# Attention stage: read-outs loaded 14 places behind their store, maxima sent by ScalarE from group 10 on, segment rows loaded one by one, more masks by VectorE

## The chip, the core and the metric

The kernel runs on one core of one Trainium2 chip. The core has TensorE (matrix products), VectorE, ScalarE, GpSimd and SyncE, each with an instruction queue of its own that is worked through in order. SyncE does nothing but issue DMAs; ScalarE can issue them as well. The metric is the device time of one execution in microseconds. Before the change the median of three runs was 810.78 us (809.48 to 811.25).

## The reference

A transformer block over 2048 tokens of width 512: a conditioned layer norm, attention with 32 heads of 16 elements in four segments of 512 tokens with a memory carried from segment to segment, the output projection with a residual, a second conditioned layer norm and a GELU network of width 1792 with a residual. The attention, cut to what matters:

```python
for s in range(N):                                   # four segments
    qs, ks, vs = q[:, :, s], k[:, :, s], v[:, :, s]
    logits = jnp.einsum("bhqd,bhkd->bhqk", qs, ks) * scale + mask     # causal
    p = _softmax(logits, axis=-1)
    a_dot = jnp.einsum("bhqk,bhkd->bhqd", p, vs)
    num = jnp.einsum("bhld,bhde->bhle", pq, M)
    den = jnp.einsum("bhld,bhd->bhl", pq, z)[..., None] + 1e-6
    o = g * (num / den) + (1.0 - g) * a_dot
    ...
x = x + ga * (o @ wo)
h = _layernorm(x, axis=-1) * (1 + cb) + sb
x = x + gb * _B_ref(h, w1, b1, w2, b2)               # GELU network
```

## The kernel before

The program has three stages: the projections for q, k and v with the memory; the attention (in the trace from about 180 to 505 us), into which the output projection of the first three segments and the first steps of the second layer norm are woven; and the GELU network. The order of the work is written out by hand.

**Groups, rounds and places.** The attention treats the 32 heads of a segment in eight groups of four heads, so there are 32 groups Q, numbered over the four segments. A group is two pairs P of two heads. The loop over the string ORDER makes one round per group; a round has 20 places, c0 to c19, between the score and exponential steps. Work that isn't part of a pair's own steps is put at a place by ap(place, function, arguments), where place 20 x R + n is cn of round R. Two entries of one place run in the order in which they were added.

**A group's own work.** Round R computes the raw scores of group R + 2 (s_part, lines 606 to 645) in six PSUM banks "att", one bank for a head of a pair or for both. VectorE takes the row maxima, either by a pass that adds the causal mask as it goes (masked_max, line 613), or by a plain reduction of both heads at once (line 617), for which TensorE has added the mask by a matmul of its own (line 645). PRM["m"] says by which way the two short score blocks of each pair go, from group 14 on (PRM["mq"]). Round R also computes the transposed scores of group R (st_part, line 693), to which three more rows of the stack qst add the negated maxima, so they can't start before these rows have landed. ScalarE takes the exponential (lines 708 and 719), GpSimd zeroes the masked triangle (line 696), and one round later, at places c11 to c18, TensorE multiplies by V (pv_part, line 733).

**Maxima.** For group Q GpSimd splits the maxima into three bf16 parts (m_rows, line 661, place 20Q - 21), TensorE transposes them (m_put, line 667, place 20Q - 13), ScalarE copies them to ms, and m_send (line 675, place 20Q - 11) issues the DMA into rows 96 to 98 of the group's stack. One exponential of 512 columns stands between m_put and m_send in the order. Group Q needs them at the beginning of round Q, 11 places later. The stacks themselves (kst and qst, line 175) are loaded at place 20Q - 65 into one of four buffers and first used at place 20Q - 40.

**Read-outs.** The result of group Q is copied to ts (ScalarE) and stored to TD at place 20Q + 42 (line 751). Two groups make a read-out U: it is loaded back in another layout at place 40U + 69, 7 places behind the second store (pv_in: dn, opk, from segment 1 on amB, in segment 3 also rm; lines 756 to 770). The divisor is inverted and scaled at 40U + 84 (den, lines 775 and 776), stored to RD at +88 (line 784), and loaded as a broadcast rbB at +96 (rb_in, line 788). At +107 the mixing multiplies and adds (lines 793 and 795, GpSimd up to read-out 12), at +117 ScalarE copies the high part (o_hi, line 127 with tile oh), at +119 GpSimd makes the low part (o_lo, line 810). Read-outs 6 and 10 make both parts 16 places later, the last two read-outs have times of their own. TensorE projects the result (wo_part, line 821) from place 242 on, two parts a round in rounds 12 to 27, four in rounds 28 to 31. VectorE adds the residual (line 839), or ScalarE and GpSimd do (line 837); the sum X2D is stored 6 places later (line 847).

**Second layer norm.** For segments 0 and 1 the four blocks of X2D are loaded again (ln2_load, line 556), measured on VectorE (561, 562), given their factor on GpSimd (148, 149), normalised (568; GpSimd in segment 0, VectorE in segment 1) and turned by TensorE (574). In segment 0 the four loads stand together at place 400, 8 places behind the last store (392); the normalisations stand at 454, 464, 474 and 484, the four turns at 493, 503, 513 and 523.

**DMAs.** All DMAs of this stage are issued by SyncE, in the order of their places; one that has to wait holds all behind it. In the order of the program the eight DMA semaphores are used in turn.

Of the kernel before, what the change touches and what calls it, by code (L numbers as in the profile page):

```python
# [27 lines left out]
PRM = {'turn': 2,  # L28
 'pv': [[31, 0, 0, 512], [36, 1, 128, 512], [37, 2, 256, 512], [38, 3, 384, 512]],
 'pvlast': [[25, 0, 0, 512], [30, 1, 128, 512], [31, 3, 384, 512], [35, 2, 256, 512]],  # L30
 'mrows': -21,
 'mput': -13,
 'stacks': -65,
 'den': [84, 84, 84, 84],
 'dnl': 11,
 'rbl': 12,
 'rdl': 4,
 'tsl': 4,
 'msl': 2,
 'xol': 6,  # L40
 'mix': 107,
 'ohi': 117,
 'olo': 119,
 'end': {'rbl': 7, 'mix': 103, 'ohi': 111, 'olo': 116},
 'wo': [[20 * i + o for i in range(8) for o in (2, 5)]] * 2 + [[20 * i + o for i in range(4) for o in (2, 5, 8, 14)]],
 'wox': -25,
 'olate': 16,
 'mixu': 13,
 'olou': 13,
 'ht': [493, 503, 513, 523],  # L50
 'ht1': 644,
 'ln': [[400, 413, 449, 454], [531, 566, 603, 624]],
 'lnl': [0, 4, 20, 34],
 'wl': [26, 66, 80, 81],
 'gate': 197,
# [18 lines left out]
 're': 'v',  # L74
 'am3': 1,
 'rme': 'p',
 'mmix': 88,
 'lnd': [[11, 10], [10, 2]],
 'mp': 0,
 'wout': ['vvvv', 'vava', 'vvvv'],  # L80
 'dens': ['p', 'p', 'p', 'v'],
 'm': [0, 0, 0, 1],
 'mq': 14,
 'pvo': ['a', 'a'],
 'mse': 'a',
# [16 lines left out]
def block_kernel(ctx: ExitStack, tc: tile.TileContext, x, wq, wk, wv, wo, betaq, betam,  # L102
                 w1, b1c, w2, b2, ccol, wmod, maskbd, mask8, out):
    nc = tc.nc
    v, act, pool, pe, sp = nc.vector, nc.scalar, nc.gpsimd, nc.tensor, nc.sync
# [57 lines left out]
    NK = 4  # L163
    qst, kst = {}, {}
# [419 lines left out]
    with ExitStack() as pb:  # L584
# [87 lines left out]
        mss = {}  # L672

        def m_send(Q):
            sp.dma_start(qst[Q % NK][96:99], mss.pop(Q))

        pts = {}
        late = []
# [227 lines left out]
        def at(P, part, f, *a):  # L906
            todo.setdefault((P, part), []).append((f, a))
# [23 lines left out]
        def ap(pos, f, *a):  # L931
            at(pos // 10, pos % 10, f, *a)
# [20 lines left out]
        for U in range(16):  # L953
            z = U // 4
            ap(40 * U + 20 + PRM["pv"][3][0] + PRM["dnl"], pv_in, U)
            if U == 15:
                ap(40 * U + 20 + PRM["pv"][3][0] + PRM["dnl"], am_in, U)
            p = {**PRM, **PRM["end"]} if U > 13 else PRM
            den_at = 40 * U + PRM["den"][z]
            ap(den_at, den, U)  # L960
            if U < 14:
                ap(den_at + PRM["rdl"], den_store, U)
            ap(den_at + p["rbl"] + (5 if U == 14 else 0), rb_in, U)
            assert 20 + PRM["pv"][3][0] + PRM["dnl"] <= PRM["den"][z] and PRM["den"][z] + p["rbl"] <= p["mix"]
            ap(40 * U + PRM["mmix"], mem_mix, U)
            ap(40 * U + p["mix"], mix, U)
            assert PRM["mmix"] <= p["mix"]
            late_by = PRM["olate"] if U in (6, 10) else 0
            ap(40 * U + p["ohi"] + late_by, o_hi, U)
            ap(40 * U + p["olo"] + late_by, o_lo, U)  # L970
            assert PRM["den"][z] <= p["mix"] <= p["ohi"] <= p["olo"]
        for s in range(NSEG - 1):
            for b in range(4):
                w = [160 * s + 240 + i for i in PRM["wo"][s][4 * b:4 * b + 4]]
# [6 lines left out]
                    ap(w[3] + 1 + PRM["xol"], wo_store, s, b)  # L981
        assert all(y[0] <= x <= y[3] < 0 for y in PRM["vl"] for x in y)
        assert PRM["wl"] == sorted(PRM["wl"]) and PRM["gate"] > PRM["wl"][1] + 60
        for i, (ln, ld) in enumerate(zip(PRM["ln"], PRM["lnd"])):
            assert ln[0] + PRM["lnl"][3] * i > 160 * i + 241 + PRM["wo"][i][15] and ln[1] > ln[0]
            assert ln[1] + 3 * ld[0] < ln[2] < ln[3] and ln[3] + 3 * ld[1] < (PRM["ht"][0], PRM["ht1"])[i]
        assert PRM["ln"][1][0] > PRM["ht"][3] and PRM["ht"] == sorted(PRM["ht"])
        def gate_load():
            sp.dma_start(gab, modD[5:6, :].to_broadcast([128, D]))

# [3 lines left out]
        at(-1, 9, swap)  # L994

        ap(PRM["gate"], gate_load)
        for i, (ln, ld) in enumerate(zip(PRM["ln"], PRM["lnd"])):
            for b in range(4):
                ap(ln[0] + PRM["lnl"][b] * i, ln2_load, i, b)
                ap(ln[1] + ld[0] * b, ln2_stats, i, b)  # L1000
                ap(ln[3] + ld[1] * b, ln2_apply, i, b, (pool, v)[i])
            ap(ln[2], ln2_rstd, i)
        for j in range(2):
            for i in range(4):
                ap(PRM["wsub"][j] + i, w_sub, j, i, v)
# [422 lines left out]
```

## Time and profile before

| | us |
|---|---|
| median of three runs | 810.78 (809.48 to 811.25) |
| the profiled execution, device time | 808.31 |
| its span, first to last instruction | 806.6 |
| TensorE busy in the span | 778.6 |
| VectorE / ScalarE / GpSimd busy | 553.5 / 476.2 / 331.8 |
| DMA queue of SyncE, share of 16 engines | 60.9% |

A page of the profile gives the busy time of each engine, slices of the span, the chain of work that ended last, and the costliest groups of instructions by line. The views named in the prediction: a list of waits (engine, line and tile that waited, what ended the wait; total us, how often, longest), stretches (busy us of each engine between two times, then the granted clock, the DMA share and GB/s), the chain of work (start, us, what), the timeline (start, us, engine, line, operation, out<-in, how many; in brackets the idle time before and what ended it), and groups by line (busy us, mean ns, idle time before). PE is TensorE, PEld its weight loads, DVE VectorE, ACT ScalarE, POOL GpSimd, SPq and ACTq the issuing of DMAs by SyncE and ScalarE. L675 is line 675 of the kernel. The end of a matmul is modelled.

### The profile page before, as it was taken

The page shows a single profiled execution, that of the slowest core. Times are in us where ns is not written, and L with a number is a line of the kernel's source. Part 1 is how long each engine was busy: PE and PEld are TensorE (multiplying, and loading weights), DVE is VectorE, ACT ScalarE, POOL GpSimd, SP SyncE. Part 2 cuts the span into 40 slices and gives each one's busy share as a digit, 9 for nine tenths or more (in the row PEclk, how much of TensorE's full clock was granted, in tenths as well). Part 3 has the DMA queues.
Part 4 walks back from the last instruction along what each step waited for, and adds up shares of the span by engine and source line. Part 5 has one row for each costly group of instructions (what it writes and reads, how often), then busy time and mean ns, then how long its engine had stood idle before and what let it go on. Part 6 is the DMA issues. An engine that isn't in the chain of part 4 may idle for free.

```text
span 806.6 us, 14065 instructions
## 1 busy us (share of the span) xinstructions
PE 778.6 (97%) x4631; PEld 539.2 (67%) x4631; DVE 553.5 (69%) x1275; ACT 476.2 (59%) x910; POOL 331.8 (41%) x554
## 2 busy tenths in 40 slices
PE   8999999999999999998989798989999999999998
PEld 4877767876545455554545455768888888888887
DVE  6686697458888877876867687867668866632523
ACT  4465545465888877775777475757745336653221
POOL 1347266451578655565875485133000404400000
PEclk9999999999999999999999999899999999999999
DMA  9596857395555667767657764585575744445443
GB/s 338 179 320 230 277 181 238 142 328 175 169 165 164 189 191 197 194 174 224 173 173 200 196 175 135 166 266 170 203 252 165 221 135 154 161 143 165 157 136 117
DMA packets 108817, 156.09 MB, mean 194 GB/s; under 512 B 16324, under 2 KB 55620, under 8 KB 108744
## 3 DMA queue, kind: packets, MB, share of 16 engines
q1 hardware_dynamic: 107880, 153.63, 60.9%
q10 hardware_dynamic: 864, 1.57, 0.5%
q8 instruction: 36, 0.59, 0.3%
q14 instruction: 37, 0.30, 0.1%
HBM read 93.95 MB, written 60.83 MB: 192 GB/s over the span
## 4 chain that ended last, share of the span: by engine, by line
PE 74%; DMA 7%; DVE 6%; ACT 4%; POOL 4%; issue 3%; SPq 1%; ACTq 0%; DVEq 0%; POOLq 0%
PE bx L1080 8%; PE att L693 7%; PE pv L733 7%; PE q L313 5%; PE bx L1345 5%; PE att L606 5%; PE by L1345 4%; PE bv L1345 4%; PE k L313 4%; PE bv L1080 4%; PE mm L821 3%; PE v L464 3%; PE spare L1345 2%; PE by L1080 2%; DMA qst<-ms 2%
## 5 line engine op out<-in xcount | busy, mean ns | idle before, releaser
L613 DVE CUSTOM_DVE_ANT_0 dump<-att,maskb 128x512 bf16<-128x512 f32 (+1 forms) x292 | 159.4, 595 | 44.6 <-PE att L606 22.0
L708 ACT ACTIVATE pt<-att 128x384 f32<-128x384 f32 (+1 forms) x256 | 124.8, 544 | 24.6 <-PE att L693 21.2
L696 POOL TENSOR_SCALAR_AFFINE_SELECT pt<-pt 128x256 f32<-128x256 f32 x256 | 103.2, 421 | 74.3 <-ACT pt L708 59.3
L693 PE MATMUL att<-qst,kst 99*128 99x256 bf16 (+3 forms) x512 | 108.3, 302 | 7.6 <-DMA qst<-ms 5.7
L693 PEld LDWEIGHTS <-kst 99*128 99x128 bf16 x512 | 43.8, 98 | 71.8 <-issue 35.9
L865 POOL TENSOR_TENSOR wb<-wa 128x256 f32<-128x256 f32 x24 | 21.4, 894 | 154.9 <-DMA wa<-in_w 144.3
L606 PE MATMUL att<-kst,qst 96*128 96x512 bf16 (+1 forms) x292 | 76.5, 344 | 3.9 <-DMA qst<-QD 3.3
L733 PE MATMUL pv<-pt,V 128*32 128x512 f32 (+1 forms) x992 | 79.6, 439 | 0.0
L719 ACT ACTIVATE pt<-att 128x256 f32<-128x256 f32 (+1 forms) x128 | 62.7, 493 | 23.2 <-PE att L693 22.7
L617 DVE TENSOR_REDUCE nm<-att 128x2 f32<-128x256 f32 (+1 forms) x110 | 56.4, 534 | 15.0 <-PE att L645 11.6
L136 DVE TENSOR_TENSOR gl<-s,gh 128x512 fp32r<-128x512 f32 x34 | 23.7, 697 | 42.1 <-ACT gh L133 42.1
L733 PEld LDWEIGHTS pv<-pt,V 128*32 128x32 f32 x992 | 25.9, 109 | 36.2 <-issue 28.1
L133 ACT ACTIVATE gh<-s 128x512 fp32r<-128x512 f32 x34 | 21.3, 628 | 46.3 <-PE spare L1345 16.7
L1085 ACT ACTIVATE s<-s,b1t 128x512 f32<-128x512 f32 x42 | 30.2, 720 | 17.9 <-DVE s L1089 17.9
L1089 DVE TENSOR_TENSOR s<-bv,s 128x512 f32<-128x512 f32 x28 | 19.2, 687 | 24.4 <-PE bv L1080 19.0
L606 PEld LDWEIGHTS <-qst 96*128 96x128 bf16 x292 | 23.7, 98 | 13.6 <-issue 7.6
L509 POOL TENSOR_TENSOR q<-qr,q 128x512 bf16<-128x512 f32 x16 | 18.7, 1168 | 27.8 <-ACT q L508 27.5
L645 PE MATMUL att<-maskb,identb 128*128 128x256 bf16 x110 | 29.9, 278 | 0.0
L500 POOL TENSOR_SCALAR qp<-qp 128x512 f32<-128x512 f32 x12 | 18.8, 1563 | 25.8 <-ACT qp L495 25.8
L136 DVE TENSOR_TENSOR w1ml<-s,w1mh 128x512 fp32r<-128x512 f32 x18 | 13.0, 721 | 22.5 <-ACT w1mh L133 22.5
L643 PE MATMUL att<-kst,qst 96*128 96x128 bf16 (+1 forms) x110 | 27.3, 248 | 0.8 <-ACT pt L708 0.8
L133 ACT ACTIVATE w1mh<-s 128x512 fp32r<-128x512 f32 x18 | 11.3, 629 | 26.8 <-PE spare L1345 11.3
(364 smaller groups left out, 2152.0 us busy)
## 6 DMA issues: line engine op xcount, KB each, us to landing
GD<-s SPq DMA_DIRECT2D x56, 256.0 KB
s<-GD SPq DMA_DIRECT2D x52, 256.0 KB
kst<-KD SPq DMA_DIRECT2D x32, 384.0 KB
qst<-QD SPq DMA_DIRECT2D x32, 384.0 KB
TD<-ts SPq DMA_DIRECT2D x32, 256.0 KB
xt<-X2D SPq DMA_DIRECT2D x28, 256.0 KB
wa<-in_w SPq DMA_DIRECT2D x28, 256.0 KB
QD<-q SPq DMA_DIRECT2D x16, 384.0 KB
```

The lines of the kernel that those rows point to most:

```text
L136: lo_eng.tensor_tensor(out=lo, in0=src, in1=hi.bitcast(F32), op=ALU.subtract)
L313: pe.matmul(ps, a[:, k, 128 * g:128 * g + 128], b[k], start=(k == 0 and i == 0), stop=(k == KB - 1 and i == 2))
L606: pe.matmul(ps, q_of(P, h, i), k_of(P, h, 128 * (i + 1)), start=True, stop=True)
L613: v.tensor_tensor_reduce(out=dump[n_dump[0] % 2][:, :n], in0=src, in1=maskb[:, 512 - n:], scale=-1.0, scalar=-4 * NEG, op0=ALU.add, op1=AL ...
L617: v.tensor_reduce(out=dst, in_=src, axis=AX.X, op=ALU.max, negate=True)
L693: pe.matmul(ps, k[:99, e, 128 * j:128 * j + 128], q[:99, e, 128 * j:512], start=True, stop=True)
L696: pool.affine_select(out=t, in_=t, pattern=pattern, compare_op=ALU.is_ge, fill=0.0, base=0, channel_multiplier=-1)
L708: act.activation(pt[:, h, :], ps[:, :n], AF.Exp, scale=0.25)
L719: act.activation(pt, pv_, AF.Exp, scale=0.25)
L733: pe.matmul(ps[32 * c:32 * c + 32, lo:hi], V[4 * s + j][:, VW * hd:VW * hd + 32], pt[:, c % 2, lo - o:hi - o], start=start, stop=stop)
L1080: pe.matmul(ps, a[:, i, k, :], b[k], start=start and k == 0 and c == 0, stop=k == 1 and c == 2, skip_group_check=not start)
L1345: pe.matmul(ps, a[:, c], w[:, lo:hi], start=(f == 0 and i == 0), stop=(last and i == 2))
```

## The change

Four things, all in the attention stage; what is computed stays the same.

1. Read-outs 0 to 10 and 12 move back: load at 40U + 76, divisor at +92, its store at +96, broadcast at +110, mixing at +120, high and low part at +130 and +132, the product with rm (mem_mix) at +100. Read-outs 11 and 13 keep the old places ("quick"), the last two theirs ("end"). The extra delay of read-outs 6 and 10 is gone. So the broadcasts of read-outs 10 and 12 (places 510 and 590) stand directly behind the loads of read-outs 11 and 13 (509 and 589).
2. From group 10 on ScalarE issues m_send, at the same place.
3. The X2D blocks of segment 0 are loaded at 388, 397, 408 and 417, measured at 420, 427, 434 and 446 (413, 424, 435, 446 before), normalised at 460, 467, 481 and 487, and turned at 498, 506, 514 and 523. For segment 1 the loads go from 531, 535, 551 and 565 to 528, 537, 548 and 568.
4. From group 14 on the score block of 256 columns of a group's first pair goes by masked_max as well, as that of the second pair did: two passes of 256 columns, no mask matmul, no reduction.

```diff
--- before.py
+++ after.py
@@ -31,26 +31,27 @@
- 'den': [84, 84, 84, 84],
- 'dnl': 11,
- 'rbl': 12,
+ 'den': 92,
+ 'dnl': 18,
+ 'rbl': 18,
  'rdl': 4,
  'tsl': 4,
  'msl': 2,
+ 'msa': 10,
  'xol': 6,
- 'mix': 107,
- 'ohi': 117,
- 'olo': 119,
- 'end': {'rbl': 7, 'mix': 103, 'ohi': 111, 'olo': 116},
+ 'mix': 120,
+ 'ohi': 130,
+ 'olo': 132,
+ 'quick': {'dnl': 11, 'den': 84, 'rbl': 12, 'mix': 107, 'ohi': 117, 'olo': 119},
+ 'end': {'dnl': 11, 'den': 84, 'rbl': 7, 'mix': 103, 'ohi': 111, 'olo': 116},
...
- 'olate': 16,
- 'ht': [493, 503, 513, 523],
+ 'ht': [498, 506, 514, 523],
- 'ln': [[400, 413, 449, 454], [531, 566, 603, 624]],
- 'lnl': [0, 4, 20, 34],
+ 'ln': [{'in': [388, 397, 408, 417], 'stat': [420, 427, 434, 446], 'rstd': 449, 'on': [460, 467, 481, 487]},
+        {'in': [528, 537, 548, 568], 'stat': [566, 576, 586, 596], 'rstd': 603, 'on': [624, 626, 628, 630]}],
...
- 'mmix': 88,
- 'lnd': [[11, 10], [10, 2]],
+ 'mmix': 100,
- 'm': [0, 0, 0, 1],
+ 'm': [0, 1, 0, 1],
@@ -672,7 +672,7 @@
         def m_send(Q):
-            sp.dma_start(qst[Q % NK][96:99], mss.pop(Q))
+            (sp if Q < PRM["msa"] else act).dma_start(qst[Q % NK][96:99], mss.pop(Q))
@@ -952,23 +952,22 @@
         for U in range(16):
-            ap(40 * U + 20 + PRM["pv"][3][0] + PRM["dnl"], pv_in, U)
+            p = {**PRM, **(PRM["end"] if U > 13 else PRM["quick"] if U in (11, 13) else {})}
+            in_at, den_at = 40 * U + 20 + PRM["pv"][3][0] + p["dnl"], 40 * U + p["den"]
+            ap(in_at, pv_in, U)
...
-            p = {**PRM, **PRM["end"]} if U > 13 else PRM
-            den_at = 40 * U + PRM["den"][z]
             ap(den_at, den, U)
             if U < 14:
                 ap(den_at + PRM["rdl"], den_store, U)
             ap(den_at + p["rbl"] + (5 if U == 14 else 0), rb_in, U)
...
-            late_by = PRM["olate"] if U in (6, 10) else 0
-            ap(40 * U + p["ohi"] + late_by, o_hi, U)
-            ap(40 * U + p["olo"] + late_by, o_lo, U)
+            ap(40 * U + p["ohi"], o_hi, U)
+            ap(40 * U + p["olo"], o_lo, U)
@@ -994,12 +994,12 @@
-        for i, (ln, ld) in enumerate(zip(PRM["ln"], PRM["lnd"])):
+        for i, ln in enumerate(PRM["ln"]):
             for b in range(4):
-                ap(ln[0] + PRM["lnl"][b] * i, ln2_load, i, b)
-                ap(ln[1] + ld[0] * b, ln2_stats, i, b)
-                ap(ln[3] + ld[1] * b, ln2_apply, i, b, (pool, v)[i])
-            ap(ln[2], ln2_rstd, i)
+                ap(ln["in"][b], ln2_load, i, b)
+                ap(ln["stat"][b], ln2_stats, i, b)
+                ap(ln["on"][b], ln2_apply, i, b, (pool, v)[i])
+            ap(ln["rstd"], ln2_rstd, i)
```

Lines that only check the order of the places are left out.

More of the change, by code (lines that the diff above doesn't have):

```diff
@@ L954, in block_kernel @@
             z = U // 4
-            ap(40 * U + 20 + PRM["pv"][3][0] + PRM["dnl"], pv_in, U)
+            p = {**PRM, **(PRM["end"] if U > 13 else PRM["quick"] if U in (11, 13) else {})}
+            in_at, den_at = 40 * U + 20 + PRM["pv"][3][0] + p["dnl"], 40 * U + p["den"]
+            ap(in_at, pv_in, U)
             if U == 15:
-                ap(40 * U + 20 + PRM["pv"][3][0] + PRM["dnl"], am_in, U)
-            p = {**PRM, **PRM["end"]} if U > 13 else PRM
-            den_at = 40 * U + PRM["den"][z]
+                ap(in_at, am_in, U)
             ap(den_at, den, U)
@@ L963, in block_kernel @@
             ap(den_at + p["rbl"] + (5 if U == 14 else 0), rb_in, U)
-            assert 20 + PRM["pv"][3][0] + PRM["dnl"] <= PRM["den"][z] and PRM["den"][z] + p["rbl"] <= p["mix"]
-            ap(40 * U + PRM["mmix"], mem_mix, U)
+            assert in_at <= den_at and p["den"] + p["rbl"] <= p["mix"]
+            mm_at = 88 if p["mix"] < 120 else PRM["mmix"]
+            ap(40 * U + mm_at, mem_mix, U)
             ap(40 * U + p["mix"], mix, U)
-            assert PRM["mmix"] <= p["mix"]
-            late_by = PRM["olate"] if U in (6, 10) else 0
-            ap(40 * U + p["ohi"] + late_by, o_hi, U)
-            ap(40 * U + p["olo"] + late_by, o_lo, U)
-            assert PRM["den"][z] <= p["mix"] <= p["ohi"] <= p["olo"]
+            assert mm_at <= p["mix"] <= p["ohi"] <= p["olo"]
+            ap(40 * U + p["ohi"], o_hi, U)
+            ap(40 * U + p["olo"], o_lo, U)
         for s in range(NSEG - 1):
@@ L983, in block_kernel @@
         assert PRM["wl"] == sorted(PRM["wl"]) and PRM["gate"] > PRM["wl"][1] + 60
-        for i, (ln, ld) in enumerate(zip(PRM["ln"], PRM["lnd"])):
-            assert ln[0] + PRM["lnl"][3] * i > 160 * i + 241 + PRM["wo"][i][15] and ln[1] > ln[0]
-            assert ln[1] + 3 * ld[0] < ln[2] < ln[3] and ln[3] + 3 * ld[1] < (PRM["ht"][0], PRM["ht1"])[i]
-        assert PRM["ln"][1][0] > PRM["ht"][3] and PRM["ht"] == sorted(PRM["ht"])
+        for i, ln in enumerate(PRM["ln"]):
+            assert all(a > 160 * i + 242 + PRM["wo"][i][4 * b + 3] + PRM["xol"] and a < c < ln["rstd"]
+                       for b, (a, c) in enumerate(zip(ln["in"], ln["stat"])))
+            assert ln["rstd"] < ln["on"][0] and ln["on"][3] < (PRM["ht"][0], PRM["ht1"])[i]
+        assert PRM["ln"][1]["in"][0] > PRM["ht"][3] and PRM["ht"] == sorted(PRM["ht"])
         def gate_load():
@@ L996, in block_kernel @@
         ap(PRM["gate"], gate_load)
-        for i, (ln, ld) in enumerate(zip(PRM["ln"], PRM["lnd"])):
+        for i, ln in enumerate(PRM["ln"]):
             for b in range(4):
-                ap(ln[0] + PRM["lnl"][b] * i, ln2_load, i, b)
-                ap(ln[1] + ld[0] * b, ln2_stats, i, b)
-                ap(ln[3] + ld[1] * b, ln2_apply, i, b, (pool, v)[i])
-            ap(ln[2], ln2_rstd, i)
+                ap(ln["in"][b], ln2_load, i, b)
+                ap(ln["stat"][b], ln2_stats, i, b)
+                ap(ln["on"][b], ln2_apply, i, b, (pool, v)[i])
+            ap(ln["rstd"], ln2_rstd, i)
         for j in range(2):
```

## The prediction

> **What bounds the kernel now.** I read the page first, then TensorE's waits, then stretches of the attention stage, then SyncE's queue around the two worst waits. Of the page and of TensorE's waits:
>
> ```profile
> PE 778.6 (97%) x4631; PEld 539.2 (67%) x4631; DVE 553.5 (69%) x1275; ACT 476.2 (59%) x910; POOL 331.8 (41%) x554
> ...
> PE att L693 <- DMA qst<-ms: 5.7, 3, 2.8
> PE att L606 <- DMA qst<-QD: 3.3, 2, 2.7
> PE pv L667 <- POOL nm L661: 1.2, 1, 1.2
> PE att L643 <- ACT pt L708: 0.8, 2, 0.6
> PE att L574 <- POOL xt L568: 0.7, 1, 0.7
> ```
>
> TensorE is the bound, so only its gaps and its own work count. The largest gaps are waits for two transfers of the attention stage: the maxima of a group (qst<-ms, line 675) and the stack of a group (qst<-QD, line 175). Both are issued by SyncE. Stretches, columns as in the page: busy us of each engine, then the granted clock, DMA share and GB/s:
>
> ```profile
> 246.62:254.68 8.06, 7.93 (x73) 3.93 (x77) 6.59 (x21) 6.82 (x16) 6.67 (x16) 1.00 0.73 209
> 262.38:270.08 7.70, 7.68 (x73) 3.90 (x77) 6.61 (x21) 6.47 (x15) 3.98 (x11) 1.00 0.76 207
> 322.17:331.00 8.83, 8.83 (x76) 4.62 (x74) 7.55 (x26) 7.05 (x15) 6.95 (x13) 1.00 0.57 152
> 376.50:379.92 3.42, 3.42 (x15) 2.01 (x14) 2.10 (x5) 0.91 (x3) 0.81 (x2) 0.50 0.74 227
> 458.40:461.90 3.50, 3.33 (x13) 2.04 (x14) 0.69 (x1) 1.26 (x3) 0.41 (x1) 0.51 0.48 133
> ```
>
> The first three are single rounds. From round 12 on a round has projection matmuls in it and takes 8.83 us, all of it TensorE's: 0.44 us for each of its 20 places. Before that it takes 7.70 us, 0.385 a place. The last two are what follows the two worst waits: the granted clock is 0.50 for about 3.4 us, so each costs another 1.7 us.
>
> Why the transfers are late is seen in SyncE's queue, here with TensorE's rows behind it:
>
> ```profile
> 363.91 0.44 SPq L175 DMA_DIRECT2D qst<-QD  x1
> 364.40 4.30 SPq L556 DMA_DIRECT2D xt<-X2D  x4
> 370.14 0.78 SPq L675 DMA_DIRECT2D qst<-ms  x1
> ...
> 371.90 0.50 PE L606 MATMUL att<-kst,qst 96*128 96x384 bf16 x2 [0.58 <-DMA qst<-QD]
> 375.17 0.66 PE L693 MATMUL att<-qst,kst 99*128 99x384 bf16 x3 [2.77 <-DMA qst<-ms]
> ...
> 438.41 0.79 SPq L675 DMA_DIRECT2D qst<-ms  x1
> 443.63 0.61 SPq L756 DMA_DIRECT2D dn<-TD  x1
> 447.55 0.44 SPq L175 DMA_DIRECT2D qst<-QD  x1
> ...
> 456.49 0.50 PE L606 MATMUL att<-kst,qst 96*128 96x384 bf16 x2 [2.69 <-DMA qst<-QD]
> 458.57 0.82 PE L693 MATMUL att<-qst,kst 99*128 99x384 bf16 x2 [1.58 <-DMA qst<-ms]
> ```
>
> At 364.40 the four segment rows stand in the queue, the fourth waiting for a store made 8 places before it; the maxima behind them leave at 370.14 and land five microseconds later. At 438.41 the read-out's load stands 4.4 us for its own store (443.63 less 439.20); the stack behind it leaves at 447.55, with the read-out's transfers ahead of it, and lands 8.9 us later. These are standing waits of SyncE:
>
> ```profile
> SPq L756 <- DMA TD<-ts: 33.3, 15, 4.3
> SPq L788 <- DMA RD<-dn: 19.4, 10, 4.7
> SPq L784 <- POOL dn L776: 16.8, 7, 4.9
> SPq L556 <- DMA X2D<-xb: 5.3, 2, 4.0
> SPq L675 <- DMA kst<-KD: 0.4, 1, 0.4
> ```
>
> The last row matters below: a send waits for a stack load with which it shares no data. I read it so: each DMA takes the semaphore of the DMA eight before it in the program's order (which is that stack's load here), and waits until that one has landed.
>
> **The change, part by part.**
>
> *Read-outs later.* The load goes from 7 to 14 places behind its store; the divisor's store stays in step with it (20 places behind the load, 19 before); the broadcast goes from 8 to 14 places behind the divisor's store, and the mixing stays 10 places behind the broadcast (11 before). Maxima, a broadcast and a read-out's store land so (start, us to landing):
>
> ```profile
> 278.87 4.78 DMA qst<-ms
> ...
> 300.45 6.12 DMA rbB<-RD
> ...
> 310.93 5.53 DMA TD<-ts
> ```
>
> 14 places are 6.2 us, 7 are 3.1: the 5.5 us are covered, SyncE's 33.3 and 19.4 us of standing mostly go. The stacks now leave ahead of the read-out's load instead of behind it. I take TensorE's 3.3 us on the stacks as gone (bounds 0 and 3.3).
>
> *Rows one by one.* The row whose store was 8 places old is now loaded 25 places after it, and no four stand together: the jam at 364.40 goes. With the sends off SyncE too, the 5.7 us on the maxima go (bounds 0 and 5.7; the third of them, 5.7 - 2.77 - 1.58 = 1.35, hung on the send at 278.87, which ScalarE now makes). With both kinds gone the two halved stretches go: 3.4 us. The ScalarE send is the third part:
>
> ```profile
> 276.87 0.27 ACT L127 ACTIVATE ms<-pv 48x128 bf16<-48x128 f32 x1
> ...
> 278.87 0.78 SPq L675 DMA_DIRECT2D qst<-ms  x1
> ...
> 3.31 2.20 ACTq L228 DMA_DIRECT2D wm<-in_wmod  x4
> ```
>
> *Sends by ScalarE.* The maxima were ready at 277.14 and left at 278.87; ScalarE sends them 1.7 us sooner. But the 22 sends (groups 10 to 31) take 0.78 us of an issuing queue each; ScalarE's four issues at the start took 0.55 each. What is queued behind them there are the exponentials, for which TensorE's banks and the masks wait. Between the copy of the maxima and the send one exponential lies, so part of the issue runs under it. Price from below: nothing, where the round has room: 8.83 less 7.05 us busy leaves 1.8. From above: 22 x 0.78 = 17.2 us. Sends 10, 11 and 12 fall into rounds without projections, where there is no room: there one more copy on ScalarE (6.82 against 6.47 busy) made the round 8.06 instead of 7.70, 0.36 more. I take 3 x 0.36 = 1.1 and nothing for the other 19, being nearest to the row of a round with projections.
>
> A send also waits for the DMA eight before it. By the new order that is mostly 19 to 33 places back, 8.4 us or more; for groups 21 and 29 it is a stack load 14 places back (6.2 us), and those landed 7.9 us (363.91 to 371.90 above) and 8.9 us after issue when jammed. Bounds 0 and 1.7 + 2.7 = 4.4; as the jams ahead of them go, I take 0.2.
>
> *More masks by VectorE.* Groups 14 to 31 lose one mask matmul each:
>
> ```profile
> 284.30 0.27 PE L644 MATMUL att<-kst,qst 96*128 96x256 bf16 x1
> 284.41 0.27 PE L645 MATMUL att<-maskb,identb 128*128 128x256 bf16 x1
> ...
> 438.83 0.42 DVE L613 CUSTOM_DVE_ANT_0 dump<-att,maskb 128x256 bf16<-128x256 f32 x1
> 439.18 0.42 DVE L613 CUSTOM_DVE_ANT_0 dump<-att,maskb 128x256 bf16<-128x256 f32 x1
> ...
> 444.12 0.69 DVE L617 TENSOR_REDUCE nm<-att 128x2 f32<-128x512 f32 x1
> ```
>
> From start to start such a matmul takes 0.11 us, so 18 x 0.11 = 2.0 us. VectorE does two masked maxima (438.83 to 439.60, 0.77) for a reduction of 0.69: 0.08 more in a round with 8.83 - 7.55 = 1.3 us of room, hidden by TensorE's own work. Were that room gone it would be 18 x 0.08 = 1.4.
>
> *Normalised rows and mixing on GpSimd.* The 1.2 and 0.7 us for GpSimd (maxima's rows, L667, and the normalised rows, L574) came where four normalisations and a mixing stand close together. They still do (places 460 to 492 instead of 454 to 484, with a mixing at 480), the turn behind them 5 places later. I take half, 0.9 (bounds 0 and 1.9).
>
> *New lateness.* Two read-outs, 11 and 13, keep the early places, so their loads, still 7 places behind their stores, now stand directly ahead of the broadcasts of read-outs 10 and 12. What the broadcast is late for:
>
> ```profile
> L793 POOL TENSOR_TENSOR opk<-opk,rbB 128x512 f32<-128x512 f32 x13 | 16.6, 1274 | 17.4 <-DMA rbB<-RD 17.4
> ...
> ACT oh L127 <- POOL opk L795: 5.3, 5, 1.9
> ```
>
> The load stands 5.5 - 3.1 = 2.4 us, three issues of about 0.6 follow, then 6.1 us to land: 10.3 us after place 509. GpSimd's mixing (place 520) is due after 4.8, stands 5.5, works 2 x 1.27, and ScalarE's copy at 530, due after 9.2, stands 3.6. In the rows ScalarE's longest such wait, 1.9, cost TensorE 0.6, so some 1.3 us are covered by the six banks; 3.6 would cost 2.3. Read-out 12 comes where no score matmuls are left and the banks reach further. For both I take 2.0 (bounds 0 and 4.6).
>
> **The sum.** Gone: 3.3 + 5.7 + 3.4 + 2.0 + 0.9 = 15.3. Added: 1.1 + 0.2 + 2.0 = 3.3. Net 12.0 from the profiled execution's 808.31 us (span 806.6): 796.3. That execution lies 2.5 below the median of the runs, 810.78, so the forecast is 798.8.
>
> **The rivals.**
>
> *Slower: ScalarE's queue stands at the sends.* If the issue isn't covered, 22 sends cost 17.2, the two semaphore waits 4.4, and the late broadcasts the 2.0: 808.3 - 15.3 + 23.6 = 816.6, at the median 819. For it: TensorE's banks come free in ScalarE's order, and one copy more in a round without projections was felt. Against: 1.8 us of room a round from round 12 on. It decides from 0.6 us a send ((15.3 - 0.2 - 2.0) / 22).
>
> The Trainium skill speaks for this rival (Perfetto Trace Analysis, section on the HWDGE DMA instruction): the issuing sequencer is free for its next instruction only when the descriptors have been generated, and the recorded span is that time. By it the 0.78 us would be ScalarE's whole; no row here shows a send on ScalarE.
>
> *The stall only moves.* Both late broadcasts cost TensorE 2.3 us, each is followed by a halved clock (1.7 each), and GpSimd's 1.9 stay: gone 14.4, added 1.1 + 0.2 + 8.0, net 5.1, at the median 805.7. For it: 4.4 us of standing at the same load at 438.41; against: with less traffic ahead the broadcast lands sooner.
>
> The halved clock in it is argued from 376.50, behind gaps of 0.58 and 2.77. The Trainium skill (TensorE: Matmul & The Clock Gate, section "What's actually happening") halves after an idle window of about 3.4 us; by that a gap of 2.3 stays warm and the rival would give 802.3. The trace halves after gaps that are shorter each, so I keep the penalty.
>
> *It doesn't do what it says.* If the stores land in 8 us rather than 5.5, as the stack at 447.55 did, 14 places don't cover them and SyncE stands as before. The sends are then off it, but stand for their semaphores: gone 2.0 + 5.7, added 1.1 + 4.4, net 2.2, at the median 808.6. Against: the 8 us were landings behind a jam.
>
> **How the numbers follow.** Forecast 0.55 (own range 794 to 802), stall moves 0.23, slower 0.13, doesn't do what it says 0.06, better than all of this 0.03. With the other 1.0 of GpSimd's waits gone too and nothing added the sum gives 808.3 - 16.3, at the median 794.5; ScalarE's 0.8 in TensorE's waits and the 1.8 us between the runs shown lead to 791.9, and I take 791 as the low end. The high end holds the moved stall with that spread: 808. A measurement of this kernel can tell about 0.2%, 1.6 us, from no change; the third rival lies at that edge and I put 0.05 of its 0.06 there: faster 0.82, same 0.05, slower 0.13.
>
> **What would show it.** Right: no row of TensorE waiting for qst<-ms or qst<-QD over 0.5 us; no stretch at clock 0.50 between 210 and 480 us; rounds of 8.7 instead of 8.83; SyncE's waits for TD and RD under 10 us each. ScalarE's waits would show the slower rival (exponentials idle behind its own issues, or sends waiting for kst and rm); the moved stall would show as ScalarE's oh waiting over 3 us around place 530, with TensorE idle behind it. Wrong would be rounds over 9 us from round 12 on.

## The result and the profile after

The changed kernel takes 808.48 us (median of 20 runs, 804.33 to 813.67), the kernel before 809.09 on the same chip (20 runs): ratio 0.9997 with a 95% interval of 0.9976 to 1.0018. That is no change, where the forecast was 1.5% faster (798.8 from 810.78). The profiled execution has a span of 806.3 us against 806.6. Most of the forecast gain is there on the way, 7.7 us by the last groups, and is given back behind them. TensorE's waits after (engine, tile and line that waited, what ended it; total us, how often, longest):

```profile
PE pv L733 <- POOL pt L696: 4.3, 2, 3.0
PE bx L1080 <- ACT s L1116: 4.1, 2, 3.9
PE att L693 <- DMA qst<-ms: 2.8, 4, 1.5
PE att L693 <- ACT pt L719: 1.8, 2, 1.6
...
PE att L574 <- POOL xt L568: 0.6, 1, 0.6
```

The stacks (qst<-QD, 3.3 before) are gone, the maxima are down from 5.7 to 2.8. In their place stand waits that the list of before did not have: the products with V wait for GpSimd's masks, a transposed score for a ScalarE exponential. Where this happens is seen in the lengths of the rounds, from one m_put (line 667) to the next, worked out from the starts in the traces; the last column is an experiment that follows below. Each kernel has one trace, so these lengths are those of one execution.

| round that begins with m_put of group | before | after | broadcasts first |
|---|---|---|---|
| 14, 16 | 8.83 | 8.73 | 8.73 |
| 13 / 15 / 17 | 8.83 / 9.55 / 8.83 | 8.91 / 9.37 / 9.21 | 8.89 / 9.23 / 9.28 |
| 21 | 14.01 | 10.57 | 9.83 |
| 27 | 8.83 | 12.06 | 8.92 |
| 29 | 16.31 | 10.69 | 10.78 |
| start of m_put of group 30, us | 463.52 | 455.86 | 450.96 |
| start of the 49th of the 64 turns of line 574, us | 567.22 | 567.34 | 555.26 |

The 49th turn lies in the first part of the GELU network. At the m_put of group 30 the changed kernel is 7.7 us ahead, although round 27 has cost it 3.2. A hundred microseconds later it is ahead by nothing. The first place, in the timeline (start, us, engine, line, operation, out<-in; in brackets the idle time before and what ended it):

```profile
412.76 0.38 SPq L751 DMA_DIRECT2D TD<-ts  x1
415.83 0.60 SPq L756 DMA_DIRECT2D dn<-TD  x1
416.48 0.58 SPq L758 DMA_DIRECT2D opk<-TD  x1
417.11 0.45 SPq L765 DMA_DIRECT2D amB<-AMD  x1
417.66 0.59 SPq L788 DMA_DIRECT2D rbB<-RD  x1
...
424.88 1.27 POOL L793 TENSOR_TENSOR opk<-opk,rbB 128x512 f32<-128x512 f32 x1 [4.58 <-DMA rbB<-RD]
...
427.52 0.63 ACT L127 ACTIVATE oh<-opk 128x512 fp32r<-128x512 f32 x1 [1.46 <-POOL opk L795]
...
428.48 0.73 PE L693 MATMUL att<-qst,kst 99*128 99x512 bf16 x2 [1.60 <-ACT pt L719]
```

SyncE's first row ends at 413.14: it stands 2.7 us at the load of read-out 11, then issues three DMAs, and only then the broadcast of read-out 10. GpSimd has nothing to do for 4.58 us, ScalarE's copy of the high part waits for GpSimd with the exponentials queued behind it, and TensorE stands 1.60. The second place is read-outs 13 and 12, at the end of the groups:

```profile
459.45 0.57 SPq L788 DMA_DIRECT2D rbB<-RD  x1
...
467.19 1.27 POOL L793 TENSOR_TENSOR opk<-opk,rbB 128x512 f32<-128x512 f32 x1 [4.59 <-DMA rbB<-RD]
...
473.44 1.43 POOL L800 TENSOR_TENSOR amB<-amB,rm 128x512 f32<-128x512 f32 x1
474.83 1.94 POOL L696 TENSOR_SCALAR_AFFINE_SELECT pt<-pt 128x256 f32<-128x256 f32 x3
...
475.47 1.05 PE L733 MATMUL pv<-pt,V 128*32 128x512 f32 x4 [1.28 <-POOL pt L696]
...
479.57 1.54 PE L733 MATMUL pv<-pt,V 128*32 128x512 f32 x4 [3.05 <-POOL pt L696]
```

Here the masks of the last groups stand in GpSimd's queue behind the mixing, and TensorE waits for them, 4.3 us in all. Both stalls are followed by a halved clock. Stretches of 3.41 us (busy us of each engine, granted clock, DMA share, GB/s):

```profile
425.39:428.80 3.41, 1.81 (x14) 0.80 (x10) 2.47 (x10) 1.96 (x5) 3.33 (x6) 1.00 0.33 106
428.80:432.21 3.41, 3.41 (x28) 1.18 (x27) 0.00 (x0) 1.39 (x4) 3.33 (x9) 0.50 0.57 130
...
476.59:480.00 3.41, 0.43 (x2) 0.14 (x4) 2.65 (x3) 0.00 (x0) 3.41 (x6) 1.00 0.09 11
480.00:483.41 3.41, 3.41 (x13) 1.53 (x9) 0.00 (x0) 1.47 (x3) 2.12 (x6) 0.50 0.58 178
```

With 1.7 us for each halved stretch the two places come to 1.60 + 1.28 + 3.05 + 2 x 1.7 = 9.3 us. A third stall lies in the start of the GELU network, which also was there before, shorter (1.40 us at 534.71 and 1.54 at 542.01):

```profile
539.90 0.60 ACT L1116 ACTIVATE s<-bx 128x512 f32<-128x512 f32 x1 [6.38 <-DMA GD<-s]
...
540.55 0.50 PE L1080 MATMUL bx<-rt2h,w1mh 128*128 128x512 f32 x1 [3.90 <-ACT s L1116]
```

### The profile page after: what moved, and what is told of

Its sections match the earlier page's. It is cut to its first block, busy times and chain, and to the rows that moved or that the text cites. A ratio compares the mean times of both kernels' runs of the same rounds, so it can differ in the third digit from the quotient of the medians.

```text
span 806.3 us, 14066 instructions
## 1 busy us (share of the span) xinstructions
PE 779.9 (97%) x4613; PEld 536.7 (67%) x4613; DVE 555.3 (69%) x1329; ACT 474.9 (59%) x910; POOL 331.8 (41%) x554
## 4 chain that ended last, share of the span: by engine, by line
PE 73%; DMA 7%; DVE 6%; POOL 6%; ACT 5%; issue 4%; SPq 0%; ACTq 0%; DVEq 0%; POOLq 0%
PE bx L1080 8%; PE pv L733 6%; PE att L693 5%; PE q L313 5%; PE bx L1345 5%; PE by L1345 5%; PE bv L1345 5%; PE att L606 4%; PE bv L1080 4%; PE k L313 4%; PE mm L821 3%; DMA qst<-ms 3%; PE v L464 3%; PE spare L1345 2%; PE by L1080 2%
## 5 line engine op out<-in xcount | busy, mean ns | idle before, releaser
L613 DVE CUSTOM_DVE_ANT_0 dump<-att,maskb 128x384 bf16<-128x384 f32 (+2 forms) x328 | 172.7, 575 | 49.6 <-PE att L606 22.8
L708 ACT ACTIVATE pt<-att 128x384 f32<-128x384 f32 (+1 forms) x256 | 127.2, 546 | 22.2 <-PE att L693 13.8
L733 PE MATMUL pv<-pt,V 128*32 128x512 f32 (+1 forms) x992 | 82.4, 446 | 4.4 <-POOL pt L696 4.3
L606 PE MATMUL att<-kst,qst 96*128 96x384 bf16 (+2 forms) x328 | 83.5, 336 | 1.3 <-DVE nm L613 0.6
L719 ACT ACTIVATE pt<-att 128x256 f32<-128x256 f32 (+1 forms) x128 | 60.6, 494 | 20.8 <-PE att L693 20.3
L617 DVE TENSOR_REDUCE nm<-att 128x2 f32<-128x256 f32 (+1 forms) x92 | 43.9, 503 | 3.6 <-PE att L645 2.6
L606 PEld LDWEIGHTS <-qst 96*128 96x128 bf16 x328 | 27.2, 98 | 13.5 <-issue 9.4
L127 ACT ACTIVATE ts<-pv 128x512 f32<-128x512 f32 x31 | 18.5, 597 | 17.9 <-PE pv L733 17.9
L613 DVE DVE_READ_ACCUMULATOR2_ANT nm<- 128x1 f32 x328 | 27.2, 83 | 0.0
```

Of the source, the lines that this page charges most:

```text
L606: pe.matmul(ps, q_of(P, h, i), k_of(P, h, 128 * (i + 1)), start=True, stop=True)
L613: v.tensor_tensor_reduce(out=dump[n_dump[0] % 2][:, :n], in0=src, in1=maskb[:, 512 - n:], scale=-1.0, scalar=-4 * NEG, op0=ALU.add, op1=AL ...
L617: v.tensor_reduce(out=dst, in_=src, axis=AX.X, op=ALU.max, negate=True)
L708: act.activation(pt[:, h, :], ps[:, :n], AF.Exp, scale=0.25)
L719: act.activation(pt, pv_, AF.Exp, scale=0.25)
L733: pe.matmul(ps[32 * c:32 * c + 32, lo:hi], V[4 * s + j][:, VW * hd:VW * hd + 32], pt[:, c % 2, lo - o:hi - o], start=start, stop=stop)
```

## The experiments

The theory: the jams were removed as forecast, and the two late broadcasts, with the halved clock behind them, cost what was gained. The rivals: ScalarE's sends cost it; the rounds gained are lost at a fixed point further on whatever comes before; one of the other parts is worth nothing. Times are medians, each ratio is to the kernel before on the same chip, with its 95% interval. The kernel before took 808.63 us beside the first four runs, 809.06 beside the next four and 809.94 beside the last four.

**Broadcasts first.** The two broadcasts go two places ahead, in front of the early loads:

```diff
-            ap(den_at + p["rbl"] + (5 if U == 14 else 0), rb_in, U)
+            ap(den_at + p["rbl"] + (5 if U == 14 else 0) - (2 if U in (10, 12) else 0), rb_in, U)
```

> The changed kernel, with the broadcasts of read-outs 10 and 12 issued one place ahead of the loads of read-outs 11 and 13 (places 508 and 588 instead of 510 and 590). Late broadcasts (theory): in the changed kernel GpSimd stood 4.6 us twice for them; these two waits fall under 2 us, round 27 (12.06 us) goes to 9 or less, TensorE's waits of 4.3 us for the masks in rounds 30 and 31 go, and the time is 4 to 8 us below the changed kernel: 801 to 805. Overload (rival): GpSimd simply has too much to do in rounds 30 and 31; only round 27 gets shorter, TensorE still waits 3 us or more for masks, time 805 to 807. Fixed end (rival): the start of the GELU network doesn't come earlier whatever the attention gains; the first turn of segment 2 stays at 567 us, time 807 to 809.

Measured 797.42 us, ratio 0.9847 (0.9817 to 0.9877): 11.1 us faster than the changed kernel. In the timeline of this kernel:

```profile
412.22 0.60 SPq L788 DMA_DIRECT2D rbB<-RD  x1
414.69 0.58 SPq L756 DMA_DIRECT2D dn<-TD  x1
...
419.18 1.30 POOL L793 TENSOR_TENSOR opk<-opk,rbB 128x512 f32<-128x512 f32 x1
...
528.49 0.64 PE L1080 MATMUL bx<-rt2h,w1mh 128*128 128x512 f32 x1 [2.04 <-ACT s L1116]
```

The broadcast leaves 2.5 us before the load instead of 1.8 behind it, the mixing has no bracket any more, round 27 is 8.92 us. GpSimd's waits for broadcasts, in the list of waits of the changed kernel and of this one:

```profile
POOL opk L793 <- DMA rbB<-RD: 12.2, 5, 4.6
```

```profile
POOL opk L793 <- DMA rbB<-RD: 2.2, 3, 1.1
```

Two changed places, and the whole forecast gain is there, more than the 4 to 8 us expected of them. The stall in the GELU network (the last line of the timeline) is 2.04 us instead of 3.90; with the 9.3 us of the two places that makes 11.2. That the late broadcasts lengthened it too is not shown. The rival of a fixed point falls with the same run: the 49th turn moved from 567.34 to 555.26.

**One broadcast at a time.** The same edit for read-out 10 alone, and for read-out 12 alone:

```diff
- (2 if U in (10, 12) else 0)
+ (2 if U in (10,) else 0)     # the other kernel: (12,)
```

> The changed kernel with the broadcast of read-out 10 alone one place ahead (508); that of read-out 12 stays behind the load of read-out 13. Each spot by itself (theory): round 27 goes from 12.06 to 9 us, rounds 30 and 31 keep their 4.3 us of waits for masks and the halved clock behind; time 3 to 4.5 us below the changed kernel, 804 to 805.5. If the late work of round 27 was also what made the end late (rival), the end gets better too, 798 to 802.

> The changed kernel with the broadcast of read-out 12 alone one place ahead (588). Each spot by itself: round 27 stays near 12 us, the waits for masks in rounds 30 and 31 go; 6 to 8 us below the changed kernel, 800.5 to 802.5. With the run for read-out 10 alone the two gains add up to the 11 us of both. If they overlap, each alone brings most of the 11 us.

Measured 801.65 (0.99, 0.9881 to 0.9919) and 802.27 (0.9902, 0.9876 to 0.9928): about 7 and 6 us faster than the changed kernel, so each late broadcast costs, and the two gains (13) add to a little more than both together (11.1). The two places aren't independent, though. With read-out 10 alone early, TensorE was to keep its 4.3 us of waits for the masks, since the broadcast of read-out 12 is still late. It keeps 0.4:

```profile
462.44 1.28 POOL L793 TENSOR_TENSOR opk<-opk,rbB 128x512 f32<-128x512 f32 x1 [2.82 <-DMA rbB<-RD]
```

```profile
PE pv L733 <- POOL pt L696: 0.4, 1, 0.4
```

The broadcast of read-out 12 leaves 1.0 us behind the m_put of group 30 there, in the changed kernel 3.6, and GpSimd stands 2.82 us for it instead of 4.59. The time lies in the range of the rival, and its account fits: part of what made the last groups late was the lateness of round 27. Part of the gain is taken by new places: rounds 29 and 30 take 13.60 and 10.40 us.

With read-out 12 alone early, round 27 was to stay near 12 us and takes 9.30, with GpSimd standing 3.38 us for read-out 10; round 28 takes 13.86:

```profile
442.48 0.66 PE L693 MATMUL att<-qst,kst 99*128 99x384 bf16 x3 [3.36 <-DMA qst<-ms]
```

So what a late broadcast costs, and where, differs between these executions. Five traces have the broadcast of read-out 10 late. GpSimd stands 4.58 us for it in the changed kernel, and 2.80 to 3.38 in the others. Behind the 4.58 TensorE waits 1.60 us for ScalarE at that place, in the others 0.41 at most; their longer waits come later, mostly for the maxima (0.91 to 3.36 us). That these come from the late broadcast as well is not shown: the run with both broadcasts early and all sends by SyncE, further on, also has one of 1.63.

**Read-out 12 early as a whole.** It gets the old places too, so that no broadcast of it follows a load:

```diff
-            p = {**PRM, **(PRM["end"] if U > 13 else PRM["quick"] if U in (11, 13) else {})}
+            p = {**PRM, **(PRM["end"] if U > 13 else PRM["quick"] if U in (11, 12, 13) else {})}
```

> The changed kernel, with read-out 12 at the early places as well (load at 549, mixing at 587), so that only read-out 10 has its broadcast behind an early load. Late broadcasts: round 27 stays at 12, the mask waits of rounds 30 and 31 go, 3 to 5 us below the changed kernel: 804 to 806. Overload: the same here, since its work leaves rounds 30 and 31 as well. Fixed end: 807 to 809. Beside the run with the broadcasts first it tells late broadcasts from overload: if that run still waits for masks in round 31 and this one doesn't, it is overload.

Measured 804.13 (0.9945, 0.9918 to 0.9971). The waits for the masks are gone, as expected; round 27, which was to stay at 12 us, is 9.09. It gains 4.4 us, less than the early broadcast alone: its trace has two other stalls, 1.17 and 2.80 us at 437 and 447, the second with the clock halved for 6.8 us.

**All sends back to SyncE**, in the changed kernel and then together with broadcasts first:

```diff
- 'msa': 10,
+ 'msa': 32,
```

> The changed kernel, with all maxima sent by SyncE again. If ScalarE's sends are worth what the prediction gave them (they take the maxima off a queue that stands), TensorE's waits for qst<-ms rise from 2.8 to 5 us or more and the time to 811 or above. If they cost what they bring (ScalarE holds exponentials back in the rounds that also copy a high part: 8.9 to 9.2 us instead of 8.73 in rounds 13, 17, 19 and 23), these rounds go to 8.75 or less, the waits for qst<-ms rise by no more than that saves, and the time is 805 to 809.

> The changed kernel with the broadcasts of read-outs 10 and 12 one place ahead of the early loads, and all maxima sent by SyncE. If the two costs are separate (11 us for the broadcasts, 4 us for ScalarE's sends), the time is 792 to 795, rounds 13, 15, 17, 19 and 23 take 8.73 us, and this is the fastest so far. If SyncE's sends were good only because the late broadcasts had slowed the rest, the time stays at 796 to 800 and TensorE's waits for qst<-ms are above 3 us.

Measured 804.21 (0.9934, 0.9909 to 0.9959) and 797.47 (0.9844, 0.982 to 0.9868). Alone the edit gains 4.3 us, beside the early broadcasts nothing. What ScalarE's sends cost is seen in the timeline of the changed kernel:

```profile
414.65 0.58 ACT L708 ACTIVATE pt<-att 128x512 f32<-128x512 f32 x1
414.78 0.73 ACTq L675 DMA_DIRECT2D qst<-ms  x1
415.56 0.60 ACT L708 ACTIVATE pt<-att 128x512 f32<-128x512 f32 x1 [0.33 <-ACT pt L708]
```

The send is issued while an exponential runs, and holds the next one for 0.33 us. In rounds that also copy a high part this shows (8.91, 9.37 and 9.21 us for rounds 13, 15 and 17; 8.73, 8.73 and 8.72 with the sends on SyncE). What SyncE's sends cost is seen in TensorE's waits with all sends on SyncE and the broadcasts late:

```profile
PE att L693 <- DMA qst<-ms: 4.9, 4, 1.5
PE pv L733 <- POOL pt L696: 4.0, 2, 3.1
```

The maxima wait 4.9 us instead of 2.8. With the broadcasts early it is 3.4 against 1.1: there the two prices about cancel, by the times. Why the edit gains 4.3 us with the broadcasts late is seen in part: GpSimd stands 3.37 us for read-out 10 instead of 4.58, and one stretch has the halved clock (478.89) instead of three, which is 3.4 us.

**ScalarE's sends from group 20 on**, with broadcasts first: SyncE sends while its queue has room, ScalarE where the segment rows and the last read-outs crowd it.

```diff
- 'msa': 10,
+ 'msa': 20,
```

> The changed kernel with the two broadcasts first, and with ScalarE sending the maxima from group 20 on instead of group 10 on. Theory: ScalarE's sends cost 0.2 to 0.5 us in rounds that have a high part to copy (about every second one), and SyncE's queue has room before the segment rows of round 19 on: 5 such rounds at about 0.3 and the two early ones at 0.3, so 2 us faster, about 795.5, with rounds 13, 15 and 17 at 8.73 us. Rival: as when all sends were given back to SyncE (797.5), a wait for the maxima turns up behind SyncE's other transfers and takes the gain: 797 to 798.

Measured 794.75 (0.982, 0.9795 to 0.9845), the fastest of all the versions, 1.8% below the kernel before. Rounds 13, 15 and 17 are at 8.73, and TensorE's waits for the maxima stay small:

```profile
PE bx L1080 <- ACT s L1116: 2.0, 2, 1.9
...
PE att L693 <- DMA qst<-ms: 1.1, 2, 0.7
```

Against broadcasts first alone it is 2.7 us by medians; the intervals of the two ratios overlap, so that this step is likely rather than shown by the times.

**The sends alone**, in the kernel before:

```diff
-            sp.dma_start(qst[Q % NK][96:99], mss.pop(Q))
+            (sp if Q < 10 else act).dma_start(qst[Q % NK][96:99], mss.pop(Q))
```

> The kernel before, with ScalarE sending the maxima from group 10 on and nothing else changed. If the sends off SyncE's queue take away most of TensorE's wait for qst<-ms and the halved clock (prediction: 5.7 + 3.4 us gone, 1.1 added), the time is 2 to 7 us below before. If the sends cost what the other sends showed (about 4 us) and wait for semaphores of transfers that stand in SyncE's queue, it is within 2 us of before or above.

Measured 805.15 (0.9954, 0.9929 to 0.9978): a gain of 3.9 us. By itself, where SyncE's queue is jammed, this part pays, though not at the maxima: in its trace TensorE's waits for them fall only from 5.7 to 4.7 us, those for the stacks from 3.3 to 0.4.

**The read-outs alone**, with broadcasts first, made from the changed kernel by taking the other three parts back:

```diff
+ ... - (2 if U in (10, 12) else 0), rb_in, U)
- 'm': [0, 1, 0, 1],
+ 'm': [0, 0, 0, 1],
-            (sp if Q < PRM["msa"] else act).dma_start(qst[Q % NK][96:99], mss.pop(Q))
+            sp.dma_start(qst[Q % NK][96:99], mss.pop(Q))
- 'ht': [498, 506, 514, 523],
+ 'ht': [493, 503, 513, 523],
- 'ln': [{'in': [388, 397, 408, 417], ...
+ 'ln': [[400, 413, 449, 454], [531, 566, 603, 624]],
```

> The kernel before with the later read-outs alone (and with the two broadcasts ahead of the early loads); sends by SyncE, segment rows together, masks as before. Theory: SyncE's standing for TD and RD falls to a third, the waits for stacks (3.3 us) and the send behind the read-out's load (1.6) go with one halved clock (1.7); the jam of the segment rows at place 400 stays with its 3.4 us and halved clock: about 6.5 us faster than before, 802.5. Rival: the sends by ScalarE are what gains (4 us when run alone), the later read-outs alone are worth under 2 us: over 807.

Measured 800.57 (0.9885, 0.986 to 0.991): 9.4 us faster than before, the largest part. SyncE's waits there:

```profile
SPq L789 <- DMA RD<-dn: 7.9, 7, 3.1
...
SPq L757 <- DMA TD<-ts: 5.9, 3, 3.1
```

They stood at 19.4 and 33.3 before. (An added line moves the numbers by one.) The expectation that the jam of the segment rows stays with all of its cost missed: that wait for the maxima is 1.57 us without a halved clock instead of 2.77 with one.

**The segment rows alone**, in the kernel before:

```diff
- 'ht': [493, 503, 513, 523],
+ 'ht': [498, 506, 514, 523],
- 'ln': [[400, 413, 449, 454], [531, 566, 603, 624]],
+ 'ln': [{'in': [388, 397, 408, 417], 'stat': [420, 427, 434, 446], 'rstd': 449, 'on': [460, 467, 481, 487]},
...
```

> The kernel before with the segment rows loaded one by one at the new places, and nothing else. Theory: the jam at place 400 goes, with TensorE's waits of 2.8 and 0.6 us and the halved clock of 1.7 behind them: about 5 us faster, 804, and no wait for the maxima over 1 us in round 20. Rival: the stall only goes on to the next jam, the read-out's load of 4.4 us: within 1.6 us of before.

Measured 805.0 (0.9947, 0.9928 to 0.9966): the time expected, and not for the reason given. In the timeline the rows leave one by one and the maxima 2.4 us after the start of round 21 (363.88) instead of 4.0 (370.14 after 366.17), and TensorE waits for them nearly as long:

```profile
362.47 0.60 SPq L556 DMA_DIRECT2D xt<-X2D  x1
...
365.80 0.42 SPq L556 DMA_DIRECT2D xt<-X2D  x1
366.32 0.79 SPq L675 DMA_DIRECT2D qst<-ms  x1
...
372.64 0.66 PE L693 MATMUL att<-qst,kst 99*128 99x384 bf16 x3 [2.43 <-DMA qst<-ms]
```

The transfer itself took six microseconds there. Round 21 is 13.75 us (14.01 before); the gain came in rounds 11, 15, 28 and 29 (1.1, 0.7, 0.8 and 1.7 us shorter). Rounds 11 and 15 come before the first moved row, so why those are shorter in the execution profiled stays open.

**The masks as before**, in the changed kernel and with broadcasts first:

```diff
- 'm': [0, 1, 0, 1],
+ 'm': [0, 0, 0, 1],
```

> The changed kernel, with the masks as before ('m' without its second one). If the masks are worth their 18 x 0.11 us, rounds without a stall go from 8.73 back to 8.83 and the time rises by 2 us to 810 or 811. If VectorE's longer passes cost as much elsewhere (maxima ready later, TensorE waiting for nm), the rounds go to 8.83 and the time stays within 1 us of the changed kernel.

> The changed kernel with the two broadcasts of read-outs 10 and 12 ahead of the early loads (797.4 us when run before), but with the masks as before the change (a mask matmul and a plain reduction for the first pair). Theory: with the stalls gone TensorE sets the time, and the 18 mask matmuls of 0.11 us are worth what the sum gave them: about 2.0 us slower than 797.4, so 799.4, rounds without a stall 8.83 instead of 8.73 us. Rival: the time that a shorter round gains is given back at the next transfer that isn't there yet, as it seemed in the changed kernel itself, where undoing the masks cost 0.7: then within 0.8 us of 797.4.

Measured 809.19 (1.0008, 0.9982 to 1.0033) and 797.65 (0.9863, 0.9839 to 0.9886; broadcasts first alone 0.9847): no loss that can be told. The rounds without a stall are 8.83 us again, and with broadcasts first the m_put of group 30 comes 2.2 us later (453.17 instead of 450.96), 1.8 of it from group 12 on, in whose round the changed masks begin. But the 49th turn comes only 0.3 later (555.59 instead of 555.26): the waits for ScalarE at the start of the GELU network are 0.8 + 0.9 us there, without a halved clock, instead of 2.0 with one. What a shorter round gains ends in that wait.

The first of these two runs shows something else. The broadcast of read-out 10 is as late there as in the changed kernel, yet round 27 takes 9.02 us:

```profile
418.49 0.59 SPq L788 DMA_DIRECT2D rbB<-RD  x1
...
424.04 1.27 POOL L793 TENSOR_TENSOR opk<-opk,rbB 128x512 f32<-128x512 f32 x1 [2.80 <-DMA rbB<-RD]
...
427.00 0.63 ACT L127 ACTIVATE oh<-opk 128x512 fp32r<-128x512 f32 x1
```

It landed 5.5 us after its issue instead of 7.2. GpSimd stood 2.8 us, ScalarE not at all: one or two microseconds of landing time made the difference between this stall and none. That execution lost the time behind it, at the maxima and at the masks of the last groups, which waited as before (1.06 and 2.52 us, the clock halved for 6.8).

## Why the prediction was wrong

**The step that failed is "New lateness".** It named the place and the mechanism: the loads of read-outs 11 and 13 ahead of the broadcasts of 10 and 12, GpSimd's mixing, ScalarE's copy, TensorE. It put GpSimd's standing at 5.5 us; it was 4.58 and 4.59. What was wrong is the price, 2.0 us "for both" with bounds of 0 and 4.6, where taking the lateness away gave 11.1. Three things were left out of the bound:

- The clock behind the stall. The step's upper bound of 4.6 holds two gaps of 2.3 and no halved stretch, although the prediction had priced one at 1.7 and used it in a rival.
- The other work in GpSimd's queue. The step followed the mixing to ScalarE's copy only. For read-out 12 it argued that "no score matmuls are left and the banks reach further"; there the waiting instruction held the masks of the last groups, and these cost 4.3 us in the changed kernel, more than read-out 10. The step also priced the two one by one, and with read-out 10 early the same place cost 0.4.
- The bound came from a row of another place: a copy that waited 1.9 cost TensorE 0.6. At 427.52 a copy waited 1.46 and TensorE 1.60.

"The stall only moves" was the rival that had it: its 2.3 + 1.7 for each broadcast make 8.0, against 9.3 read in the gaps. Its sign in the profile, ScalarE's oh waiting over 3 us around place 530, didn't appear (1.46), TensorE's idle time behind it did. The sign of being wrong, rounds over 9 us from round 12 on, could not tell: they stood in the kernel before too (9.55 in round 15). The rival's forecast of 805.7 was still 0.6% below the kernel before, the result 0.03%; what the terms below missed lies between them.

**Read-outs later** was right, and the largest part: the stacks' 3.3 us are gone, and the part alone with broadcasts first gave 9.4. One of its signs in the profile was wrong. SyncE's waits for TD and RD were to fall under 10 us each; in the changed kernel

```profile
SPq L175 <- PE att L693: 66.6, 25, 5.7
...
SPq L788 <- DMA RD<-dn: 32.8, 11, 6.4
...
SPq L756 <- DMA TD<-ts: 10.1, 5, 3.5
```

the wait for TD fell from 33.3 to 10.1, but that for RD rose from 19.4. SyncE, without the sends that had paced it, comes to every DMA sooner and waits there; with all sends back on SyncE it was 8.1. Such a wait costs only if what stands behind it is due.

**The maxima's 5.7 us** were taken as gone, with no wait over 0.5 us; 2.8 were left, and the longest of those shows why. ScalarE sent those maxima at 365.86, as soon as they were copied, and they still held TensorE until 372.50 (1.49). Before, SyncE sent them at 370.14 and TensorE was held until 375.17. The jam was part of the lateness, the slow transfer at a DMA share of 1.0 the other part. **The 3.4 us of halved clock** behind the two old stalls went as forecast, and three new halved stretches (428.8, 480.0 and 541.4) took their place. A third old one, 6.83 us at 502.80, which the sum left out, went as well, so the halved time between 200 and 780 us fell from 13.7 to 10.2, worth 1.7.

**Sends by ScalarE** were 1.1 in the sum, for groups 10 to 12 alone, and "nothing for the other 19". Group 10's round is 8.06, 0.3 over the 7.75 of before, as forecast. The rounds with a high part pay too: 0.18, 0.64, 0.48 and 0.19 us over 8.73 in rounds 13, 15, 17 and 19, 1.5 together, of which 0.3 is a wait for the maxima. The rival "ScalarE's queue stands at the sends" took 0.78 for each; the send lay under an exponential and held the next by 0.33. By the rule that the prediction quoted from the Trainium skill (Perfetto Trace Analysis, section on the HWDGE DMA instruction) the queue is held for the recorded span; the rows agree, since the next exponential starts 0.05 us behind the send's 0.73, but most of that span was covered.

**More masks by VectorE**: 0.10 us a round, as forecast (0.11), and 1.8 us by group 30. At the end of the kernel nothing of it is left, since the wait at the start of the GELU network grows by about as much. The step looked at the rounds and never at what comes behind the stage. **GpSimd's waits** of 1.9 us fell by 1.3 (0.9 forecast); the last normalisation stands at place 487, not at 492 as the prediction has it. The new waits for the masks, 4.3, are more than that.

## What to carry to other kernels

Where an in-order queue issues DMAs, moving most of a series later and leaving a few early puts the early ones, which have to wait, directly ahead of others that are now due: look at each neighbour in the new order, not only at what the moved step itself needs. Price a stall by everything that stands behind the waiting instruction on its engine, and by the clock that follows, before calling it covered. Parts that gain alone don't add: here 1.2, 0.5 and 0.5% made 1.5% together, and the masks' nearly 2 us vanished in a wait further on.

## What the runs showed of the hardware

The clock halves on a fixed grid. In every trace the halved stretches lasted 3.41 us (or two of these, 6.83; one at the very end is cut off by the end of the trace), and their starts lie whole multiples of that apart: 428.80, 480.00 and 541.44 in the changed kernel are 15 and 18 times 3.413 apart. What goes with a halved stretch in these traces is how busy TensorE was in the 3.41 us of the grid before, more than the length of a single gap. The stretch of 425.39 above had 1.81 us of work (0.53) and a gap of 1.60: halved. This one had a gap of 1.49:

```profile
370.78:374.19 3.41, 1.92 (x14) 1.16 (x13) 2.49 (x9) 1.72 (x4) 1.27 (x5) 1.00 1.02 255
374.19:377.61 3.42, 3.42 (x28) 1.70 (x25) 2.79 (x9) 2.16 (x5) 0.85 (x3) 1.00 0.67 217
```

At 1.92 us (0.56) the clock stayed at 1.00. Laying the grid over the traces of before, after and the twelve experiments, from 200 to 780 us: all 25 stretches with a busy share under 0.50 were followed by a halved one, of ten between 0.50 and 0.534 eight were, and of some 2,300 above that only three, each of which was itself halved, so that its matmuls took longer. (Busy shares go by the modelled ends of the matmuls.) The Trainium skill (TensorE: Matmul & The Clock Gate, section "What's actually happening") has the window of 3.41 us and that it runs freely; the traces agree with both. It gives an idle window as the condition; here half a window of idle time was enough. So in this kernel, where TensorE has work for the whole halved stretch, a stall of 1.7 us or more that falls into one window costs another 1.7 us, and one that lies across two windows can cost less.
